# Strassen's form in a second matrix product, for two of a chunk's eight pairs of rows

## The chip, the cores and the metric

The kernel runs on one core of a Trainium2 chip. The metric is the device time of one execution in microseconds; the median of three runs of the kernel before is 2169.81 us (2168.5 to 2170.58). The profile shows one further execution. Its engines are PE (TensorE: matmuls, and PEld, its weight loads), DVE (VectorE), ACT (ScalarE), POOL (GpSimd) and SP (SyncE), whose queue issues nearly all DMAs. Matmuls write to PSUM, in banks of 2 KB per partition, 512 columns of float32.

## The reference, cut to what matters

```python
def _attn_ref(q, k, v, tau):                  # B, N, C = 4, 6080, 256
    qn = q / (norm(q, axis=1) + 1e-06);  kn = k / (norm(k, axis=1) + 1e-06)
    s = kn.transpose(0, 2, 1) @ qn / tau      # 256 x 256 for each batch, summed over N
    a = softmax(s)
    return v @ a                              # x: 24320 tokens of 256

def _moe_ref(x, w_in, w_out):                 # w_in 256 x 2048, w_out 2048 x 256
    h = x @ w_in
    g = h * (1.0 / (1.0 + np.exp(-1.702 * h)))
    return g @ w_out
```

All of it is float32; w_in and w_out arrive as float64 and are cut to float32 on the chip.

## The kernel before

For each batch the kernel multiplies a (the softmax) into w_in, so that h = v @ (a w_in). This is the first product. Tokens lie in the columns: a chunk is 1024 tokens (960 in the last one of a batch), halved into two columns of blocks of 512 (480); six chunks for each of four batches make 24. The 16 blocks of 128 rows of h are taken as 8 pairs, and a pair of row blocks, two halves of the inner 256 and two halves of the tokens are the 2 x 2 blocks of Strassen's form (Winograd's variant): 7 block products instead of 8. `unit` (L784) makes one pair: products P1 to P7 go into the banks X, Y and Z of PSUM, ACT copies partial sums out of X (`snap`, s1, u2, u4), DVE adds them (`add`, c11, c22, c21) and ACT applies the gate in place (`gate`). There are 24 x 8 = 192 units.

Every operand is split in two float32r parts, a high one (a cast) and a low one (`low`, the difference), and each block product is three matmuls: high x high, high x low, low x high. So a unit's first product has 21 matmuls.

The second product is the plain form: for each of a pair's two row blocks, each half of the tokens and each of two output blocks, three matmuls (L867) are summed in one of four banks psO0 to psO3, which a chunk holds from its first pair to its last: 24 matmuls a pair. Its operands are the gated rows' parts gh and gl, and wo_h and wo_l, which lie in SBUF for the whole run. At the end of a chunk DVE copies two of the banks and ACT the other two into the tile osb, and two DMAs store it (L889 to L901). `values` (L732) makes the seven operands of v for a chunk, `operands` (L675) those of the folded weights for a pair; the latter are kept in DRAM (w_ops) and loaded again for each unit (`weights_again`). The next batch's squares, scores and softmax run beside the products of the batch before; the first batch's stand at the start.

The order of the instructions is made by a list scheduler, `Plan.order` (L89): each node has an engine, a cost in ns, dependences, buffer slots and a due number; when an engine is free, the scheduler takes the available node of the lowest due number. `DUE` (L193) holds offsets to these numbers, `FILL` says how many blocks of the next batch's scores go beside which unit of the first chunk. Each engine then runs its list in order; so does SP's queue, in which a DMA that waits for its slot holds up what is queued behind it. The slots of one name are reused in turn: three for w_op, one for osb.

Of the kernel before, what the change touches and what calls it, by code (L numbers as in the profile page):

```python
# [11 lines left out]
F32 = mybir.dt.float32  # L12
F32R = mybir.dt.float32r
# [170 lines left out]
def dve(n):  # L184
    return (151 + n) / 0.96


def dve_fast(n):
# [10 lines left out]
}  # L199

LAG = 3200

FILL = {"gap": 10, "0": 4, "1": 3, "2": 6, "3": 0, "4": 6}
# [8 lines left out]
def channel_attention_then_glu(  # L212
# [60 lines left out]
    ident = sb.tile([P, P], F32, name="ident")  # L273
    tau_sb = sb.tile([P, 64], F32, name="tau_sb")[:, :1]
    rtau = sb.tile([P, 64], F32, name="rtau")[:, :1]
    wo_h = sb.tile([P, NF, C], F32R, name="wo_h")
    wo_l = sb.tile([P, NF, C], F32R, name="wo_l")
    win_f = dr.tile([NC2, P, DFF], F32, name="win_f")
    NK = 7
    w_ops = dr.tile([2, NU, P, NK, 2, P], F32, name="w_ops")  # L280

# [27 lines left out]
    g.add("DVE", 60, lambda: nc.vector.memset(half, 0.5), due=-8e9)  # L309
    const_i = g.add("POOL", 2000, lambda: make_identity(nc, ident), due=-9e9)  # L310
# [87 lines left out]
    wo_ready = {}  # L398

    def wout_convert(grp, words, due, slot, lows):  # L400
        t, n = to_float32(slot, lows, words, due)
        fs = slice(FG * grp, FG * (grp + 1))
        flat = lambda w: w[:, fs, :].rearrange("p f d -> p (f d)")
        h = cast(lambda: flat(wo_h), lambda: t(), FG * C, [n], [t], due + 7)
        l = low(lambda: flat(wo_l), lambda: t(), lambda: flat(wo_h), FG * C, [h], [t], due + 8)
        for f in range(FG * grp, FG * (grp + 1)):
            wo_ready[f] = l
# [3 lines left out]
    class Attention:  # L411
# [53 lines left out]
        def scores(self, us, S, due, each=25, direct=False):  # L465

            prev = None
            for n_, u in enumerate(us):
# [5 lines left out]
                if not direct:  # L474
                    hl = sbuf("hl", [P, 2, UT, 2, C], F32R, "qks")
                    part = lambda h, hl=hl, pp=pp, nt=nt: hl()[:pp, :, :nt, h, :]
                    at_ = due + each * (n_ - len(us))
                    n = cast(lambda part=part: part(0), src, w, ready, [raw, hl], at_)
                    ready = [n, low(lambda part=part: part(1), src, lambda part=part: part(0), w, [n], [raw, hl], at_ + 3)]
                for j in range(nt):  # L480
# [3 lines left out]
                    def fn(j=j, first=first, last=last, hl=hl, pp=pp):  # L484
# [19 lines left out]
                        due + (each * n_ + 3 * j if direct else j), kind="f" if direct else C,  # L504
# [25 lines left out]
        def fill(self, us, slots, due, load_due, bank_):  # L530

            for u, slot in zip(us, slots):
                self.load_unit(u, load_due, slot)
            return bank_, self.scores(us, bank_, due, 6, True), due + 6 * len(us)

        def norms(self, due):

            self.xd = xd = sbuf("acc", [P, 2, NC2, C], F32, "x_dq")
            self.rn = rn = small("rn", 2 * NC2)
            diag = lambda: xd()[:, 1, 0, :].rearrange("p (i x) -> p i x", i=NC2)  # L540
# [23 lines left out]
            self.rn_n = g.add("DVE", 800, fn_b, [a, const_i], [rn, xd], due + 4)  # L564

        def spread(self, due):

            xd, rn = self.xd, self.rn
            diag = lambda: xd()[:, 1, 0, :].rearrange("p (i x) -> p i x", i=NC2)
# [3 lines left out]
            def fn_c():  # L573
                for i in range(NC2):
                    nc.tensor.matmul(
                        pb()[:, i * P : (i + 1) * P], lhsT=ones, rhs=diag()[:, i, :], start=True, stop=True,
                    )

            c = g.add("PE", 440, fn_c, [self.rn_n], [pb, xd], due, kind="f")
# [7 lines left out]
        def softmax(self, due):  # L587
# [9 lines left out]
            for i in range(NC2):  # L597
                xi, mi, zi = (lambda i=i: xd()[:, 0, i, :]), (lambda i=i: mx()[:, i : i + 1]), (lambda i=i: zs()[:, i : i + 1])

                def fn_s(i=i, xi=xi, mi=mi):  # L600
                    nc.vector.scalar_tensor_tensor(
                        xi(), in0=S()[:, i * C : (i + 1) * C], scalar=rn()[:, NC2 + i : NC2 + i + 1], in1=self.rqb(),
                        op0=ALU.mult, op1=ALU.mult,
                    )
                    nc.vector.reduce_max(mi(), xi(), axis=AX.X)
                    nc.vector.tensor_scalar_mul(mi(), mi(), -1.0)

                e = g.add("DVE", 1000, fn_s, [*self.factors, self.last], [S, xd, rn, mx], due + 2 * i)
                e = g.add(
                    "ACT", 700 if i else 2000,  # L610
                    lambda xi=xi, mi=mi, zi=zi: nc.scalar.activation(xi(), xi(), AF.Exp, bias=mi(), accum_out=zi()),
                    [e], [xd, mx, zs], due + 2 + 2 * i,
                )

                def fn_z(xi=xi, zi=zi):
                    nc.vector.tensor_scalar_add(zi(), zi(), 1e-9)
                    nc.vector.reciprocal(zi(), zi())
                    nc.vector.tensor_scalar_mul(xi(), xi(), zi())

                z = g.add("DVE", 700, fn_z, [e], [xd, zs], due + 3 + 2 * i)  # L620

                def fn_t(i=i):
                    for j in range(NC2):
                        nc.tensor.transpose(
                            ptv()[:, j, i * P : (i + 1) * P], xd()[:, 0, i, j * P : (j + 1) * P], ident,
                        )

                ts.append(g.add("PE", 440, fn_t, [z], [xd, pt], due + 4 + 2 * i, kind="f"))
# [46 lines left out]
    def operands(at, p, w0, w1, ready, due, slot, sums):  # L675
# [13 lines left out]
        for k, z, src, deps, uses in (  # L689
# [9 lines left out]
        at.stored[p] = g.add(  # L699
            "SP", 50 + 896 * 2.6, lambda: nc.sync.dma_start(w_ops[at.b % 2, p], wt().bitcast(F32)), ok, [wt], due + 20, lag=LAG,  # L700
        )
# [30 lines left out]
    def values(b, c, turn, due, use, after=()):  # L732
# [4 lines left out]
        vt = sbuf("vt", [P, 4, HALF], F32, "v_t")  # L737
        src = vT[b, :, o : o + w].rearrange("(c p) n -> p c n", p=P)
        r = load(lambda: raw()[:, :, :w], src, 1024, after, [raw], due - 25)
        B = lambda j, n: raw()[:, j, n * hw : (n + 1) * hw]  # L740
        t = lambda i: vt()[:, i, :hw]
        t1 = tt(lambda: t(0), lambda: B(0, 1), lambda: B(0, 0), ALU.subtract, hw, [r], [raw, vt], due)
        t3 = tt(lambda: t(1), lambda: B(0, 1), lambda: B(1, 1), ALU.subtract, hw, [r], [raw, vt], due + 12)
        t2 = tt(lambda: t(2), lambda: B(1, 1), lambda: t(0), ALU.subtract, hw, [t1], [raw, vt], due + 24)
        t4 = tt(lambda: t(3), lambda: B(1, 0), lambda: t(2), ALU.subtract, hw, [t2], [raw, vt], due + 36)
        out, ok = {}, {}
        for n, (m, what, src, dep, use_) in enumerate((
            (P1, "m1", lambda: B(0, 0), r, raw),
            (P2, "m2", lambda: B(1, 0), r, raw),
            (P6, "m6", lambda: t(2), t2, vt),  # L750
            (P5, "m5", lambda: t(0), t1, vt),
            (P7, "m7", lambda: t(1), t3, vt),
            (P3, "m3", lambda: B(1, 1), r, raw),
            (P4, "m4", lambda: t(3), t4, vt),
        )):
            v = sbuf(f"v{m}{turn if m in TWICE else ''}", [P, 2, HALF], F32R, "v_op")
            at_ = due + 48 + 24 * n if m in TWICE else use + DUE[what] - 20
# [10 lines left out]
    outs = {}  # L768

    def parting(os, d, n, ob, last, o, hw, due):  # L770
# [4 lines left out]
        ns = [  # L775
            cast(lambda: to(0), lambda: src(0), h, [last], [ob, os], due, psum=True),
            g.add("DVE", dve(h), lambda: nc.vector.tensor_copy(to(1), src(1)), [last], [ob, os], due),
        ]
# [5 lines left out]
    def unit(W, V, b, c, p):  # L784
# [6 lines left out]
        begin, end = p == 0, p == NU - 1  # L791
# [52 lines left out]

        def split(h, deps, slot, by):
            gh = sbuf("gh" + slot, [P, NCH], F32R, "gh")
            gl = sbuf("gl" + slot, [P, NCH], F32R, "gl")
# [4 lines left out]
        r1 = split(h1, [g11, g12], f"1{D % 2}", cast)  # L852
        r2 = split(h2, [g2], f"2{D % 2}", cast if D < NU else cast_v)
# [175 lines left out]
```

## Time and profile before

| | |
|---|---|
| median of three runs | 2169.81 us |
| the profiled execution | 2167.3 us |
| its span, first to last instruction | 2165.5 us |
| PE busy | 2157.9 us, 9920 instructions |
| DVE busy | 1493.9 us, 2014 instructions |
| ACT busy | 1282.7 us, 1906 instructions |
| moved by DMA | 328.72 MB, mean 152 GB/s |
| clock granted to PE | full in all slices |

Busy time is the union of an engine's instructions, and matmuls overlap in the pipeline, so PE's busy time tells that it is never empty and not how fast it goes. The median lies 2.5 us above the profiled execution.

### The profile page before, as it was taken

What the parts mean: (1) busy time and instruction counts of PE and PEld (TensorE: products, weight loads), DVE (VectorE), ACT (ScalarE), POOL (GpSimd) and SP (SyncE); (2) the same over time, 40 slices, a digit from 0 to 9 for tenths busy, and PEclk for the clock granted to TensorE, in tenths of its full rate; (3) what the DMA queues carried; (4) which work ended last, traced back from release to release, by engine and by line L of the source; (5) the groups of instructions that cost most, each with busy time, mean ns of one, the idle gap of its engine ahead of it and who ended that gap; (6) DMA issues with size and microseconds to landing.
All of it is one profiled execution on the core that took longest, in us unless ns stands there. A gap on an engine that the chain in (4) does not pass through costs nothing.

```text
span 2165.5 us, 25948 instructions
## 1 busy us (share of the span) xinstructions
PE 2157.9 (100%) x9920; PEld 1811.7 (84%) x9920; DVE 1493.9 (69%) x2014; ACT 1282.7 (59%) x1906; POOL 5.7 (0%) x10
## 2 busy tenths in 40 slices
PE   9999999999999999999999999999999999999999
PEld 8888888888888888888888888888888888888887
DVE  7898677667667676776766767677677566566554
ACT  5567666656656565665665656566566555555553
POOL 0000000000000000000000000000000000000000
PEclk9999999999999999999999999999999999999999
DMA  9755445435543433433554434243355333333331
GB/s 350 291 174 197 163 154 189 140 105 196 187 162 139 141 141 116 163 122 114 205 185 148 139 131 159 101 157 120 128 194 191 112 128 117 105 126 120 105 105 54
DMA packets 88284, 328.72 MB, mean 152 GB/s; under 512 B 9312, under 2 KB 11744, under 8 KB 88160
## 3 DMA queue, kind: packets, MB, share of 16 engines
q1 hardware_dynamic: 88016, 326.93, 43.3%
q8 instruction: 78, 1.28, 0.2%
q14 instruction: 46, 0.38, 0.0%
q10 hardware_dynamic: 144, 0.13, 0.0%
HBM read 270.66 MB, written 56.36 MB: 151 GB/s over the span
## 4 chain that ended last, share of the span: by engine, by line
PE 97%; DVE 1%; DMA 1%; SPq 0%; issue 0%; ACT 0%; POOL 0%; DVEq 0%; ACTq 0%
PE ps_o L867 48%; PE ps_X L801 24%; PE ps_Y L801 12%; PE ps_Z L801 6%; PE ps_s L496 3%; PE ps_w L666 2%; PE ps_s L490 1%; DVE acc L297 1%; DMA raw_qk<-in_k 1%; DMA words<-in_w_in 0%; SPq L288 0%; DVE wf L297 0%; DVE low L378 0%; PE ps_n L549 0%; ACT wf L348 0%
## 5 line engine op out<-in xcount | busy, mean ns | idle before, releaser
L801 PE MATMUL ps_X<-v_op,w_op 128*128 128x512 f32 (+1 forms) x2304 | 625.4, 388 | 0.0
L867 PE MATMUL ps_o<-gh,wo_h 128*128 128x512 f32 (+1 forms) x1536 | 595.4, 388 | 0.0
L867 PE MATMUL ps_o<-gl,wo_h 128*128 128x512 f32 (+1 forms) x1536 | 595.1, 387 | 0.0
L867 PE MATMUL ps_o<-gh,wo_l 128*128 128x512 f32 (+1 forms) x1536 | 595.1, 387 | 0.0
L302 DVE TENSOR_TENSOR gl<-h,gh 128x1024 fp32r<-128x1024 f32 (+1 forms) x384 | 465.7, 1213 | 142.8 <-ACT gh L291 136.3
L801 PEld LDWEIGHTS ps_X<-v_op,w_op 128*128 128x128 f32 x2304 | 430.8, 188 | 86.0 <-ACT s L291 0.5
L291 ACT COPY s<-ps_X 128x512 f32<-128x512 f32 (+1 forms) x384 | 223.3, 582 | 258.8 <-PE ps_X L801 195.1
L817 ACT ACTIVATE h<-h 128x512 f32<-128x512 f32 (+3 forms) x384 | 319.5, 839 | 49.5 <-DVE h L297 49.0
L867 PEld LDWEIGHTS ps_o<-gl,wo_h 128*128 128x128 f32 x1536 | 288.3, 188 | 57.7
L867 PEld LDWEIGHTS ps_o<-gh,wo_h 128*128 128x128 f32 x1536 | 288.4, 188 | 56.7
L867 PEld LDWEIGHTS ps_o<-gh,wo_l 128*128 128x128 f32 x1536 | 288.4, 188 | 56.6
L801 PE MATMUL ps_Y<-v_op,w_op 128*128 128x512 f32 (+1 forms) x1152 | 322.4, 388 | 0.0
L801 PEld LDWEIGHTS ps_Y<-v_op,w_op 128*128 128x128 f32 x1152 | 214.9, 188 | 42.6 <-DVE h L297 0.3
L291 ACT CAST gh<-h 128x1024 fp32r<-128x1024 f32 (+1 forms) x200 | 208.4, 1042 | 53.3 <-PE ps_o L867 48.8
L294 DVE CAST gh<-h 128x1024 fp32r<-128x1024 f32 (+1 forms) x184 | 126.3, 687 | 138.4 <-ACT h L817 137.5
L291 ACT COPY u<-ps_X 128x512 f32<-128x512 f32 (+1 forms) x192 | 111.6, 581 | 177.0 <-DVE h L297 165.3
L297 DVE TENSOR_TENSOR h<-ps_Z,s 128x512 f32<-128x512 f32 (+1 forms) x192 | 131.3, 684 | 119.6 <-ACT s L291 105.0
L817 ACT ACTIVATE h<-ps_X 128x512 f32<-128x512 f32 (+1 forms) x192 | 114.0, 594 | 141.7 <-PE ps_X L801 139.3
L297 DVE TENSOR_TENSOR h<-ps_Y,u 128x512 f32<-128x512 f32 (+1 forms) x192 | 131.3, 684 | 92.7 <-PE ps_Y L801 90.0
L297 DVE TENSOR_TENSOR h<-ps_Y,s 128x512 f32<-128x512 f32 (+1 forms) x192 | 130.4, 679 | 59.9 <-ACT s L291 59.5
L801 PE MATMUL ps_Z<-v_op,w_op 128*128 128x512 f32 (+1 forms) x576 | 161.5, 389 | 0.0
L297 DVE TENSOR_TENSOR acc<-acc,sq 128x1024 f32<-128x1024 f32 (+2 forms) x96 | 112.9, 1176 | 21.5 <-ACT sq L457 19.4
(82 smaller groups left out, 1396.5 us busy)
## 6 DMA issues: line engine op xcount, KB each, us to landing
w_op<-w_ops SPq DMA_DIRECT2D x184, 896.0 KB, 4.6
raw_qk<-in_q SPq DMA_DIRECT2D x114, 256.0 KB, 5.2
raw_qk<-in_k SPq DMA_DIRECT2D x114, 256.0 KB, 5.4
w_ops<-w_op SPq DMA_DIRECT2D x32, 896.0 KB, 5.6
v_raw<-in_vT SPq DMA_DIRECT2D x20, 1024.0 KB, 7.1
out_T<-osb SPq DMA_DIRECT2D x39, 512.0 KB, 7.3
wf<-win_f SPq DMA_DIRECT2D x12, 512.0 KB, 6.4
words<-in_w_out SPq DMA_DIRECT2D x8, 512.0 KB, 6.0
```

What stands on the lines that cost most here:

```text
L291: return g.add("ACT", act(n, psum), lambda: nc.scalar.copy(dst(), src()), deps, uses, due)
L294: return g.add("DVE", dve_fast(n), lambda: nc.vector.tensor_copy(dst(), src()), deps, uses, due)
L297: return g.add("DVE", dve(n), lambda: nc.vector.tensor_tensor(dst(), a(), b(), op=op), deps, uses, due)
L302: lambda: nc.vector.tensor_tensor(dst(), src(), hi().bitcast(F32), op=ALU.subtract),
L490: nc.tensor.matmul(out, lhsT=hl()[:pp, 1, j, ci], rhs=hl()[:pp, 0, j, :], start=begin, stop=last, skip_group_check=True,)
L496: nc.tensor.matmul(out, lhsT=hl()[:pp, 1, j, l, ci], rhs=hl()[:pp, 0, j, r, :], start=begin and m == 0, stop=last and m == 2, skip_group_c ...
L666: nc.tensor.matmul(pb()[:, x * width : (x + 1) * width], lhsT=aT()[:, l, j, ci], rhs=wi()[:, r, o : o + width], start=x == 0 and n == 0, s ...
L801: nc.tensor.matmul(of(into), lhsT=wt()[:, m, l, :], rhs=v[m]()[:, r, :hw], start=begin and n == 0, stop=True, skip_group_check=True,)
L817: "ACT", act(n, psum), lambda: nc.scalar.activation(dst(), src(), AF.Gelu_apprx_sigmoid),
L867: nc.tensor.matmul(of(ob), lhsT=l[:, f, ds], rhs=rr()[:, n * hw : (n + 1) * hw], start=begin and i == 0 and m == 0, stop=end and i == 1 an ...
```

## The change

In all chunks but the first, the last two of the eight pairs (pairs 6 and 7) come first, and their second product takes Strassen's form as well. The inner 512 rows of the two pairs are split in the first and the second row block of each pair, the tokens in two halves and the output in two blocks of 128: with both pairs summed in the same banks, a block product is 3 x 2 = 6 matmuls, and there are seven. The units of these two pairs write their gated rows into two tiles of the pair of pairs, g_a and g_b; DVE makes four differences in place (one in g_t), ACT casts seven operands and DVE makes their seven low parts, all 1024 wide. P1 goes into the bank psO1 and is copied out by ACT into osb; P6, P5 and P3 are added on in the same bank, with copies after P6 and P5; P2 goes into psO0, P7 and P4 into psO2. The six other pairs are then added onto the same banks by the plain form, and at the chunk's end three of the four banks are summed with what lies in osb (DVE) and one is copied (ACT).

w_out's parts no longer stay in SBUF. The plain pairs' parts are written to DRAM once (wo_ops, 512 KB for each pair) and loaded again for each chunk (w_o); the seven operands of pairs 6 and 7 likewise (wj_ops), in three loads of 512 KB and one of 256 KB for a chunk (w_oj). All share four slots in SBUF. Three further edits go with it: `values` makes its differences in place, `spread` multiplies float32r parts, and the softmax of the batches after the first is done for both halves at once. The tables DUE, FILL are others; the core of the diff:

```diff
-    "m1": 13, "s1": -46, "m2": 16, "m6": 42, "u2": -46, "c11": -3, "g11": 22, "m5": 28, "u4": -4,
+    "m1": -16, "s1": -89, "m2": 50, "m6": 44, "u2": -64, "c11": -4, "g11": 193, "m5": 58, "u4": -39,
...
+NWO = 4
...
+    def wout_again(p, due):
+        w = wo_tile([P, 2, 2, C], "w_o")
+        return w, [load(lambda: w().bitcast(F32), wo_ops[p], 512, [wo_stored[p]], [w], due)]
...
+        for x, (k, z) in enumerate(((0, 2), (6, 7), (4, 6), (2, 4))):
+            w = wo_tile([P, 2, MS, 2, P], "w_oj")
+            n = load(lambda w=w, k=k, z=z: w()[:, : z - k].bitcast(F32), wj_ops[:, k:z], 256 * (z - k), stored, [w], due + 8 * x)
...
+            l1 = part(P1, "1", B11, G11, A, cast)
+            l2 = part(P2, "2", B21, G2, B_, cast)
+            t1 = tt(B11, B12, B11, ALU.subtract, n_, [*G12, l1], [A], at("ta"))
+            t2n = tt(T2, B22, B11, ALU.subtract, n_, [t1, *G2], [A, B_, t2], at("tb"))
+            part(P6, "6", T2, [t2n], t2, cast)
+            t3 = tt(B12, B12, B22, ALU.subtract, n_, [t1, *G2], [A, B_], at("tc"))
+            part(P7, "7", B12, [t3], A, cast)
+            part(P5, "5", B11, [t1], A, cast)
+            t4 = tt(B21, B21, T2, ALU.subtract, n_, [t2n, l2], [B_, t2], at("td"))
+            part(P3, "3", B22, G2, B_, cast)
+            part(P4, "4", B21, [t4], B_, cast)
...
+            os = out.os()
...
+            def snap(d, n, dep, what):
+                dst = lambda: os()[:, d, n * hw : (n + 1) * hw]
+                return dst, cast(dst, lambda: of(O[1]), hw, [dep], [O[1], os], at(what), psum=True)
+
+            m1 = product(P1, "1", O[1], True, [])
+            s1, s1n = snap(0, 0, m1, "k1")
+            m2 = product(P2, "2", O[0], True, [])
+            m6 = product(P6, "6", O[1], False, [s1n])
+            u2, u2n = snap(1, 0, m6, "k2")
+            m7 = product(P7, "7", O[2], True, [])
+            m5 = product(P5, "5", O[1], False, [u2n])
+            u4, u4n = snap(1, 1, m5, "k4")
+            c22 = tt(u4, lambda: of(O[2]), u4, ALU.add, hw, [u4n, m7], [O[2], os], at("kc"))
+            m3 = product(P3, "3", O[1], False, [u4n])
+            m4 = product(P4, "4", O[2], False, [c22])
...
-                if d == 0:
+                if sum_:
+                    ns.append(tt(to, src, to, ALU.add, hw, last, [ob, os], due_))
+                elif d == 0 and n == 0:
...
-            c, p = divmod(s, NU)
-            grp, a = divmod(p, PAIRS)
+            c, x = divmod(s, NU)
+            joint = b > 0 or c > 0
+            p = (x - MS) % NU if joint else x
+            grp, a = divmod(x, PAIRS)
...
+            if joint and x == MS - 1:
+                J.products(b, c, due, wj)
```

Where the instructions stand. First SP's queue at the end of a chunk of the last batch, before. w_op are the folded weights of a unit, out_T the stores of a chunk's outputs.

```order
L288 DMA v_raw_16374<-in_vT 128x2x1024 [waits DMAHW1_49,DVE_49]
L288 DMA w_op_16438<-w_ops_71 128x1792 [waits DMAHW6_49,DMAHW2_49,PE_49]
L288 DMA w_op_16522<-w_ops_71 128x1792 [waits DMAHW7_49,PE_49]
L899 DMA out_T<-osb_16502 128x1024 [waits DVE_49]
L899 DMA out_T<-osb_16502 128x1024 [waits Activation_49]
L288 DMA w_op_16600<-w_ops_71 128x1792 [waits DMAHW0_49,PE_49]
L288 DMA w_op_16672<-w_ops_71 128x1792 [waits DMAHW2_49,PE_49]
```

The same place now, on SP; w_oj and w_o are the operands of w_out.

```order
L296 DMA w_op_17159<-w_ops_70 128x1792 [waits DMAHW7_49,DMAHW6_49,PE_49]
L296 DMA w_oj_17233<-wj_ops_72 128x1024 [waits PE_49]
L296 DMA w_op_17244<-w_ops_70 128x1792 [waits DMAHW1_49,DMAHW0_49,PE_49]
L296 DMA w_oj_17312<-wj_ops_72 128x1024 [waits PE_49]
L1082 DMA out_T<-osb_16737 128x1024 [waits DMAHW2_49,DVE_49,Activation_49]
L1082 DMA out_T<-osb_16737 128x1024 [waits DMAHW3_49,DVE_49]
L296 DMA w_op_17354<-w_ops_70 128x1792 [waits DMAHW4_49,PE_49]
L296 DMA w_o_17398<-wo_ops_71 128x1024 [waits DMAHW5_49,PE_49]
```

A load of w_out's operands stands right ahead of the two stores, where a load of w_op stood before. Its slot (w_oj_17312) is the one that PE frees with the chunk's last matmul.

ACT's list at the same place, before: the copies into osb_16502 are those of the chunk's end, and the one wait for a DMA in it is for the store of the chunk before.

```order
L291 CAST gh_16495<-h1_16406 128x1024 [waits PE_49,Activation_49]
L817 ACTIVATE h1_16497<-h1_16497 128x512 [waits DVE_49]
L291 COPY osb_16502<-ps_o_15945 128x512 [waits DMAHW2_49,PE_49]
L291 COPY osb_16502<-ps_o_15956 128x512 [waits PE_49]
L291 COPY u2_16529<-ps_X_16441 128x512 [waits DVE_49,PE_49]
L817 ACTIVATE h2_16479<-h2_16479 128x1024
```

ACT's list now, at the start of the next chunk: osb_17385 is this chunk's tile, ps_o_17317 its bank psO1 after P1 and then after P6.

```order
L299 COPY u2_17356<-ps_X_17236 128x512 [waits DVE_49,PE_49]
L982 ACTIVATE h2_17301<-h2_17301 128x1024
L299 CAST gh_17364<-h1_17256 128x1024 [waits PE_49,Activation_49]
L299 COPY s1_17374<-ps_X_17236 128x512 [waits DVE_49,PE_49]
L299 COPY osb_17385<-ps_o_17317 128x512 [waits DMAHW3_49,DMAHW2_49]
L982 ACTIVATE h1_17362<-h1_17362 128x512
L299 CAST gh_17396<-g_b_17134 128x1024 [waits PE_49]
L299 COPY s1_17400<-ps_X_17308 128x512 [waits DVE_49]
L299 COPY osb_17385<-ps_o_17317 128x512 [waits PE_49]
```

The first copy into osb now stands at the start of a chunk and waits for two DMAs; a gate, a cast and a copy of other units are queued behind it. And the start of SP's queue before:

```order
L288 DMA raw_qk<-in_q 128x256 x2
L288 DMA raw_qk<-in_k 128x256
L288 DMA raw_qk<-in_q 64x256
L288 DMA raw_qk<-in_k 64x256
L288 DMA raw_qk<-in_q 128x512
```

The start of the same queue now:

```order
L296 DMA words<-in_w_out 128x2x512 x2
L296 DMA raw_qk<-in_q 128x256 x2
L296 DMA raw_qk<-in_k 128x256
L296 DMA raw_qk<-in_q 64x256
L296 DMA raw_qk<-in_k 64x256
```

Two loads of w_out's words, 512 KB each, now stand ahead of the first q and k.

## Rows read from the trace of the kernel before

**Rows 1.** The page, part 1: busy us (share of the span) and instructions.
```profile
PE 2157.9 (100%) x9920; PEld 1811.7 (84%) x9920; DVE 1493.9 (69%) x2014; ACT 1282.7 (59%) x1906; POOL 5.7 (0%) x10
```
**Rows 2.** Waits of PE, whole span: us in total, times, longest us.
```profile
PE ps_s L490 <- DMA raw_qk<-in_k: 1.1, 2, 0.6
PE ps_x L317 <- DVE half L309: 1.1, 1, 1.1
PE ps_n L549 <- DVE acc L297: 0.9, 1, 0.9
```
**Rows 3.** Chain of waits in order of time: start us, us, what.
```profile
1709.47 4.56 PE ps_o L867 x21
...
1809.59 4.76 PE ps_o L867 x21
```
**Rows 4.** Groups by line and form: count, busy us, mean ns; idle before.
```profile
L867 PE MATMUL ps_o<-gh,wo_h 128*128 128x512 f32 x1280 | 498.6, 390 | 0.0
...
L302 DVE TENSOR_TENSOR gl<-h,gh 128x1024 fp32r<-128x1024 f32 x320 | 391.6, 1224 | 114.6 <-ACT gh L291 109.2
...
L291 ACT CAST gh<-h 128x1024 fp32r<-128x1024 f32 x168 | 176.5, 1051 | 41.1 <-PE ps_o L867 37.1
...
L297 DVE TENSOR_TENSOR h<-ps_Y,s 128x512 f32<-128x512 f32 x160 | 109.6, 685 | 54.5 <-ACT s L291 54.1
...
L294 DVE CAST gh<-h 128x1024 fp32r<-128x1024 f32 x152 | 105.2, 692 | 115.4 <-ACT h L817 114.9
...
L291 ACT COPY osb<-ps_o 128x512 f32<-128x512 f32 x38 | 22.3, 586 | 11.9 <-PE ps_o L867 11.5
```
**Rows 5.** Busy us of each engine in three stretches, clock, DMA share, GB/s.
```profile
20.00:26.00 6.00, 5.50 (x27) 4.53 (x25) 4.47 (x5) 3.94 (x5) 0.00 (x0) 1.00 1.04 411
85.00:189.00 104.00, 103.97 (x493) 87.00 (x492) 89.51 (x134) 72.29 (x109) 0.00 (x0) 1.00 0.57 208
...
1749.00:1831.00 82.00, 82.00 (x365) 68.19 (x365) 48.67 (x61) 43.82 (x67) 0.00 (x0) 1.00 0.35 119
```
The columns after the stretch's length are PE, PEld, DVE, ACT, POOL.

**Rows 6.** Timeline of SP's queue: issue start us, us, DMA.
```profile
7.76 0.43 SPq L288 DMA_DIRECT2D words<-in_w_out  x1
...
532.41 0.91 SPq L899 DMA_DIRECT2D out_T<-osb  x2
...
1764.05 0.32 SPq L288 DMA_DIRECT2D w_op<-w_ops  x1
1764.42 0.90 SPq L899 DMA_DIRECT2D out_T<-osb  x2
```
**Rows 7.** out_T, issue to landing: from 520 to 545, 1755 to 1775, all.
```profile
DMA to landing us min/median/max: 2.6/3.1/3.7
...
DMA to landing us min/median/max: 7.0/8.1/9.1
...
DMA to landing us min/median/max: 2.0/7.3/9.6
```
**Rows 8.** The page, part 6: DMA issues, count, KB each, median us to landing.
```profile
w_op<-w_ops SPq DMA_DIRECT2D x184, 896.0 KB, 4.6
...
words<-in_w_out SPq DMA_DIRECT2D x8, 512.0 KB, 6.0
```
**Rows 9.** Timeline of PE, the first 50 us.
```profile
4.63 13.02 PE L490 MATMUL ps_s<-raw_qk 128*128 128x256 f32 x52
18.27 7.14 PE L490 MATMUL ps_s<-raw_qk 128*128 128x256 f32 x32 [0.62 <-DMA raw_qk<-in_k]
25.92 24.46 PE L490 MATMUL ps_s<-raw_qk 128*128 128x256 f32 x112 [0.50 <-DMA raw_qk<-in_k]
```
**Rows 10.** Timeline of the last microseconds.
```profile
2160.76 0.39 PE L867 MATMUL ps_o<-gl,wo_h 128*128 128x512 f32 x1
...
2161.19 0.37 ACT L291 COPY osb<-ps_o 128x256 f32<-128x256 f32 x1 [0.99 <-PE ps_o L867]
...
2161.59 0.42 DVE L777 COPY osb<-ps_o 128x256 f32<-128x256 f32 x1 [0.34 <-ACT osb L291]
```

More of the change, by code (lines that the diff above doesn't have):

```diff
@@ L193 @@
 DUE = {
[5 rows of a table removed]
[7 rows of a table added]
 }
 LAG = 3200
-FILL = {"gap": 10, "0": 4, "1": 3, "2": 6, "3": 0, "4": 6}
+NWO = 4
+SPLIT = {"from": 7}
+FILL = {"gap": 11, "0": 3, "1": 3, "2": 4, "3": 7, "4": 13}
 def width_cost(n):
@@ L280, in channel_attention_then_glu @@
     w_ops = dr.tile([2, NU, P, NK, 2, P], F32, name="w_ops")
+    MS = PAIRS
+    JOINT = list(range(NU - MS, NU))
+    wo_ops = dr.tile([NU - MS, P, 2, 2, C], F32, name="wo_ops")
+    wj_ops = dr.tile([P, NK, MS, 2, P], F32, name="wj_ops")
     def two(ap, w):
@@ L596, in softmax @@
             ts = []
[L597 to L612, printed above, removed]
-                )
[L615 to L628, printed above, removed]
@@ new lines, in softmax, with each @@
+            steps = [[i] for i in range(NC2)] if self.b == 0 else [list(range(NC2))]
+            def each(fn, idx):
+                return lambda: [fn(i) for i in idx]
+            for x, idx in enumerate(steps):
+                m = len(idx)
+                e = g.add("DVE", 1150 * m, each(fn_s, idx), [*self.factors, self.last], [S, xd, rn, mx], due + 2 * x)
+                e = g.add("ACT", 720 * m + (0 if x else 1350), each(fn_e, idx), [e], [xd, mx, zs], due + 2 + 2 * x)
+                z = g.add("DVE", 850 * m, each(fn_z, idx), [e], [xd, zs], due + 3 + 2 * x)
+                ts.append(g.add("PE", 220 * m, each(fn_t, idx), [z], [xd, pt], due + 4 + 2 * x, kind="f"))
@@ L673, in project, with sevens @@
         return pb, n
-    def operands(at, p, w0, w1, ready, due, slot, sums):
+    def sevens(w0, w1, ready, due, slot, sums, stored):
         (t0, v0), (t1, v1) = w0, w1
@@ L768, in channel_attention_then_glu, with gh_slot, __init__, os @@
     outs = {}
-    def parting(os, d, n, ob, last, o, hw, due):
+    gh_turn = [0]
+    def gh_slot():
+        gh_turn[0] += 1
+        return str(gh_turn[0] % 4)
+    class Outs:
+        def __init__(self, b, c):
+            self.banks = [bank(f"psO{i}", "o") for i in range(2 * NC2)]
+            self.prev = [None] * 4
+            self.also = [[], [], [], []]
+            self.sums = [False] * 4
+            self.tile = None
+        def os(self):
+            if self.tile is None:
+                self.tile = sbuf("os", [P, NC2, NCH], F32, "osb")
+            return self.tile
@@ L772, in parting @@
+    def parting(os, d, n, ob, last, o, hw, due, sum_):
         h = hw // 2
@@ L774, in parting @@
         src = lambda x: ob()[:, x * h : (x + 1) * h]
[L775 to L778, printed above, removed]
+        if sum_:
+            whole = lambda: os()[:, d, n * hw : (n + 1) * hw]
+            ns = [tt(whole, lambda: ob()[:, :hw], whole, ALU.add, hw, last, [ob, os], due)]
+        else:
+            ns = [
+                cast(lambda: to(0), lambda: src(0), h, last, [ob, os], due, psum=True),
+                g.add("DVE", dve(h), lambda: nc.vector.tensor_copy(to(1), src(1)), last, [ob, os], due),
+            ]
         dst = outT[d * P : (d + 1) * P, (B - 1) * N + o + n * hw : (B - 1) * N + o + (n + 1) * hw]
@@ L877, in unit @@
             return
-        os = sbuf("os", [P, NC2, NCH], F32, "osb")
+        os = out.os()
         for d in range(NC2):
@@ L881, in unit @@
             for n in range(2):
-                ob, last = outs[b, c][2 * d + n]
+                r = 2 * d + n
+                ob, last = out.banks[r], [out.prev[r], *out.also[r]]
+                sum_ = out.sums[r]
                 if b == B - 1 and c == NCHUNK - 1 and d == NC2 - 1:
-                    parting(os, d, n, ob, last, o, hw, due + 84)
+                    parting(os, d, n, ob, last, o, hw, due + 84, sum_)
                     continue
```

259 lines of the change are left out of this document (186 added, 73 removed), and 10 rows, old and new, of the table DUE.

## The prediction, made before the changed kernel was run

> **What bounds the kernel now.** I read the busy shares first: PE is busy for 2157.9 of 2165.5 us, DVE for 69% and ACT for 59% [rows 1]. Then the waits of PE itself: three rows, 3.1 us together, all in the start of the program [rows 2]; so nothing that DVE, ACT or a DMA does makes PE late once the first products run. Then the chain of waits in order of time, for the price of a matmul: in the steady part 21 matmuls of 512 columns take 4.76 us, 0.2267 us each, and 21 of 480 columns take 4.56 us, 0.2171 us each [rows 3]. The mean of 390 ns by form [rows 4] is the length of one in the pipeline and prices nothing, since the next one starts 0.2267 us later. The kernel's time is therefore the number of matmuls times their pitch, plus a start and a tail; and a change pays what it takes off PE, less what it makes PE wait.
>
> **The matmuls removed.** A pair's second product has 2 rows x 2 halves x 2 output rows x 3 terms = 24 matmuls; in Strassen's form it has 7 x 3 = 21. Two pairs of a chunk save 6, and all chunks but the first have the new form: 23 x 6 = 138, of which 19 chunks x 6 = 114 are 512 wide and 4 x 6 = 24 are 480 wide. 114 x 0.2267 = 25.84 and 24 x 0.2171 = 5.21: 31.05 us off PE. The order of the instructions shows the same 138 fewer on PE and no other difference of weight there (the spread matmuls of four batches, 8 small ones, change form).
>
> By the Trainium skill, "TensorE: Matmul & The Clock Gate", section "Back-to-back issue gap", an isolated warm matmul takes N/2.4 + 2.5 ns, 215.8 and 202.5 ns here, and the sum would be an estimated 29.5 us. Rows 3 say 226.7 and 217.1, and the sum above goes by them.
>
> **The elementwise work added.** Per chunk of the new form (512 wide) DVE gets 7 low parts where two pairs had 4, four differences of 1024, four sums out of PSUM where it had two copies, and loses two casts: 3 x 1.22 + 4 x 1.22 + 4 x 0.69 - 2 x 0.69 - 2 x 0.69 = 8.5 us. ACT gets 7 casts where it had 2, and four copies where it had two: 5 x 1.05 + 2 x 0.59 = 6.4 us [rows 4]. Over 23 chunks that is 197 us and 148 us, all beside PE if the engines have room. In the last batch DVE is busy for 48.67 us of an 82 us chunk, and becomes 57 of 80.6 (six matmuls fewer); in the first chunk, the tightest stretch, it has 89.51 of 104 us [rows 5] and gets a part of the next chunk's preparation and the seven forms of two pairs of w_out, some 6 us by the order: 92%. Nowhere does it pass PE, so I cost this at nothing; if its cover is gone in the first chunk, the price is at most what is added there, 6 us.
>
> **A wait that is added: the output tile.** Before, the tile osb is written at the end of a chunk only, and its store has a whole chunk to land. Now the first of Strassen's products of the next chunk, P1, is copied out of its bank into the same osb, and the bank goes on to P6 only after that copy. The copy waits for both stores of the chunk before. I count on the orders: after the last matmul of a chunk (call its end L) stand 39 matmuls up to the first one of P6 in the last batch, 39 x 0.2267 = 8.84 us; over the 23 boundaries this is 6.8 to 10.2 us, 8.84 in eight of them and 6.8 in two. Behind it must go: PE's drain, 0.2 us (a matmul's start at 2160.76 plus its pitch, to ACT's start at 2161.19 [rows 10]); the DVE sum, 0.69 [rows 4]; the issue of two stores, to about L + 1.1, since the second issue follows the first by 0.45 us [rows 6]; the landing, x; the copy, 0.59 [rows 4]; and 0.2 again for PE. So P6 is late only if x is over 8.84 - 1.1 - 0.8 = 6.9 us. What x will be no row shows, because what is queued ahead is new: a load of 512 KB (w_oj), issued at L when PE frees its slot. Two ends: with nothing ahead the two stores landed in 2.6 and 3.7 us; with a load of 896 KB issued 0.4 us ahead of them, in 7.0 and 9.1 [rows 6, 7]. I go by the share of bytes, 512/896 of the way from 3.7 to 8.1 (the middle of that pair): 6.2 us, under 6.9. Behind ACT's waiting copy stand in its queue the gate, cast and copy of other pairs, which feed PE some 2 us later, so a late landing is passed on and not gained back. I take 0.2 us for a boundary on average (the two with 6.8 us lose 1.3 each, and a few where batch loads stand ahead lose some): +4.6 us. The ends: 0, and 9.1 - 6.9 = 2.2 us each, 51 us.
>
> By the Trainium skill, "DMA: Bandwidth & Descriptors", section "Queues, rings and completion order", each DMA engine takes the descriptors of one issuing engine's ring in order. That speaks against this change, since w_oj stands ahead of the stores; rows 7 agree (7.0 to 9.1 us behind a load, against 2.6 to 3.7 with one issued after them). By it the stores pay the load's whole transfer, which the share of bytes above has in it.
>
> **Loads of w_out's operands.** SP issues 238 loads and stores more, in one queue; each waits for PE to free its slot, and what is queued behind waits with it. A slot is free on PE 6.8 us or more ahead of the operand's first use, save in four places (the first load after the P products, beside the batch's loads), where 21 matmuls or 4.7 to 4.8 us stand between. A load of 896 KB landed in 4.6 us and one of 512 KB with strided rows in 6.0 [rows 8]. I take a quarter of a microsecond each, +1; the ends are 0 and 4 x (6.0 + 0.3 - 4.7), 6.
>
> **Start and tail.** The two loads of w_out's words now go ahead of q and k: 1 MB, some 2.5 us at 411 GB/s [rows 5]. But PE waits there for data anyway: its runs of 52 and 32 matmuls end in waits of 0.6 and 0.5 us, at 17.65 and 25.41 [rows 2, 9], and the words stood at 7.76 us in the same queue [rows 6], ahead of the data that ended the second of them. One MB moves within the stretch that data bound: +0.5, ends -1 and +3. In the tail a sum of 0.69 takes the place of two half copies, 0.37 + 0.42 [rows 4, 10]: -0.1, which I leave out.
>
> **Sum.** -31.05 + 0 + 4.6 + 1 + 0.5 = -25 us. The profiled execution took 2167.3 us (span 2165.5 and 1.8 around it): 2142.3. The median of the runs shown, 2169.8, lies 2.5 above it, and on that scale I predict 2145 us.
>
> **Rivals.**
> (a) The store decides. If the stores land in over 6.9 us at every boundary, each boundary loses the excess. At 8.25 us it is 23 x 1.35 = 31: the gain is gone; beyond that the kernel is slower: at 9.1, 51 - 31 = +20, 2190 us with the other terms at nothing. For it: 7.3 us is the median of all stores before [rows 7]. Against: those had 896 KB ahead, now 512. At 7.5 us (half way to the point where it decides) 14 us go, and the time is 2154.
> (b) DVE becomes the bound where a batch's attention runs beside the products. 17 of the 23 chunks carry it; were each to lose 1 us, the time is 2162. For it: 86% in the first chunk before [rows 5], and chains through both ACT and DVE that are longer than any there was. Against: PE has no wait there today at that 86% [rows 2].
> (c) No difference: what PE loses is given back by waits of (a) and (b) together, 31 us, 2170.
> (d) Nothing waits at all, and the start gains: 2169.8 - 31 - 1 = 2138.
>
> **Chances.** The forecast with its neighbours (d) and the small form of (a), 2136 to 2156: 0.74. (b), and (a) between 7.5 and 8 us, 2156 to 2165: 0.13. (c), within 0.2% (about what a measurement of this kernel tells from no change, 4.3 us): 0.06. (a) in full, slower: 0.07. So faster 0.87, same 0.06, slower 0.07. The range reaches from (d) with a margin to most of (b): 2135 to 2162, which leaves out some 0.18.
>
> **What would show it.** In the profile after: PE with 138 matmuls fewer and the same pitch (4.76 for 21); DVE near 1690 us and ACT near 1430 us busy; PE still without rows of idle of any weight, or, if (a), idle time of PE at the P6 products, with ACT's osb copies ended by the DMA out_T, near 1 us and more each; if (b), PE's idle spread over products and ended by DVE or ACT. The time is wrong if the stores land in over 8 us, or if the pitch of the new products (the same weights twice in a row, other operands) is not 0.2267.

## The result, and the profile after

The changed kernel takes 2143.22 us (median of 4 runs, 2142.41 to 2146.37), the kernel before 2170.18 (4 runs, 2168.5 to 2170.58): a ratio of 0.988, with the interval 0.9863 to 0.9897. The prediction was 2145. The profiled execution took 2142.4 us with a span of 2140.6, 24.9 us less than before; the sum had said 2142.3.

The page after, part 1 (busy us, share, instructions), answers to [rows 1]:

```profile
PE 2131.3 (100%) x9774; PEld 1785.7 (83%) x9774; DVE 1659.3 (78%) x2199; ACT 1409.6 (66%) x2078; POOL 6.4 (0%) x10
```

PE has 146 instructions fewer: the 138, and 8 of the 16 spread matmuls. DVE's busy time rose by 165 us and ACT's by 127. The work is still what I had added up, 197 and 148: by the lengths of their instructions, added one by one, DVE has 198.0 us more (1767.3 after 1569.3) and ACT 150.4 (1523.7 after 1373.3). Neighbouring instructions overlap (ACT's copy at 1150.94 takes 0.58 us, and its next instruction starts at 1151.42), and busy time counts an overlap once.

PE's waits (us in total, times, longest), which answer to [rows 2]:

```profile
PE ps_s L535 <- DMA raw_qk<-in_q: 2.0, 1, 2.0
PE ps_o L904 <- ACT osb L299: 1.2, 2, 0.8
PE ps_x L326 <- DVE half L317: 1.1, 1, 1.1
PE ps_X L966 <- ACT u L299: 0.6, 1, 0.6
```

The waits of its weight loads show a late operand earlier, since they run ahead of the matmul; of that view one row counts here:

```profile
PEld ps_o L904 <- ACT osb L299: 2.5, 3, 1.2
```

The waits are still few, and one of them is the wait that the prediction added: a Strassen product (L904) behind the copy into osb. The 0.6 us behind u is the same wait passed on: at 211.75 us ACT starts the copy into osb after 1.20 us of waiting for out_T, and the copy u stands behind it. The price of a matmul is as before [rows 3]; the chain has, in the order start us, us, what:

```profile
358.04 2.04 PE ps_o L1046 x9
...
373.00 2.72 PE ps_o L904 x12
```

2.04 / 9 and 2.72 / 12 are both 0.2267 us, in the plain form and in the new one. (By the Trainium skill, "TensorE: Matmul & The Clock Gate", section "Back-to-back issue gap", the gap of an isolated matmul would be 0.2158; the measurement decides.)

**Where the 31.05 us went.** The timeline of PE gives the start of every run of matmuls, and the order gives what stands ahead of it. Ahead times pitch, taken from the start, is PE's lateness; I followed it through both programs. Up to 160 us it grows by 1.05 us more after than before. At chunk boundaries it does not grow before; after, it grows at seven of 23: 0.93, 0.55, 0.65, 0.68, 1.13, 0.76 and 0.82 us, 5.5 together. The rest, the changes of batch and the eight spread matmuls, comes 0.4 us cheaper. 31.05 - 1.05 - 5.5 + 0.4 = 24.9. The sum is firm, its split only to about 1 us: with the lateness read at every single matmul, and each boundary taken around its Strassen products alone, the start costs 1.2, the seven places 4.5 (the three of the store, 0.93, 1.13 and 0.82 above, 2.8 of it), and the rest is 0.5 dearer.

Three of the seven places, at the start of chunks 1, 12 and 21, end with the store. ACT's timeline of the change at the last two (start us, us, operation; in brackets the idle time before it and what ended it):

```profile
1150.94 0.58 ACT L299 COPY osb<-ps_o 128x512 f32<-128x512 f32 x1 [1.53 <-DMA out_T<-osb]
...
1917.68 0.58 ACT L299 COPY osb<-ps_o 128x512 f32<-128x512 f32 x1 [1.58 <-DMA out_T<-osb]
```

The view of out_T has the landing of these two boundaries' stores, and last that of all stores, which answers to [rows 7]:

```profile
DMA to landing us min/median/max: 6.7/7.1/7.4
...
DMA to landing us min/median/max: 6.9/7.3/7.7
...
DMA to landing us min/median/max: 2.0/5.5/7.7
```

The later of the two stores decides. Where it takes 7.4 and 7.7 us PE is late; at the usual 5.3 to 6.1 the copy waits 0.41 us at most, and PE hardly. The prediction put the point at 6.9 for a room of 8.84: chunk 21 has that room, its store lands 0.8 us over the point, and PE is 0.82 late. At chunk 1 the landing was 6.2; there the store was issued late, 1.5 us after the chunk's last matmul and not 1.1, since ACT's queue was full and its copy of the chunk's end (204.92) came late. The two long landings are not a chance of one execution: they stand at the same two boundaries in the runs words_later (7.8 and 7.9) and own_words (7.6 and 7.9) below. At chunk 21 SP issues the same DMAs as at the boundaries before and after it, so why the stores take longer there no run tells.

The start in PE's timeline:

```profile
6.83 5.80 PE L535 MATMUL ps_s<-raw_qk 128*128 128x256 f32 x14 [2.00 <-DMA raw_qk<-in_q]
```

And in the table of stretches (length, PE, PEld, DVE, ACT, POOL, granted clock, DMA share, GB/s):

```profile
6.00:8.00 2.00, 1.17 (x5) 0.83 (x6) 0.00 (x0) 0.17 (x1) 0.00 (x0) 1.00 1.09 347
8.00:10.00 2.00, 2.00 (x6) 1.18 (x7) 0.00 (x0) 1.99 (x2) 0.00 (x0) 0.59 0.99 369
10.00:12.00 2.00, 2.00 (x6) 1.17 (x5) 1.00 (x2) 2.00 (x4) 0.00 (x0) 0.50 0.51 148
...
16.00:18.00 2.00, 2.00 (x11) 1.77 (x10) 1.76 (x3) 1.49 (x3) 0.00 (x0) 1.00 1.05 405
```

The first q now comes at 6.83 instead of 4.63 us [rows 9], and after that wait PE runs for some 7 us at the lower of its two clocks, 1.2 GHz (0.50): 14 matmuls take 5.80 us. The waits at 18.27 and 25.92 [rows 9] are gone in exchange. The clock does not follow from the wait alone. The run low_planned below has the same wait and keeps the higher clock, 2.4 GHz (1.00 from 8 to 20 us):

```profile
6.83 6.75 PE L535 MATMUL ps_s<-raw_qk 128*128 128x256 f32 x28 [2.00 <-DMA raw_qk<-in_q]
```

### The profile page after: what moved, and what is told of

It reads as the page before. It is cut to its first block, busy times and chain, and to the rows that moved or that the text cites. A ratio compares the mean times of both kernels' runs of the same rounds, so it can differ in the third digit from the quotient of the medians.

```text
span 2140.6 us, 26818 instructions
## 1 busy us (share of the span) xinstructions
PE 2131.3 (100%) x9774; PEld 1785.7 (83%) x9774; DVE 1659.3 (78%) x2199; ACT 1409.6 (66%) x2078; POOL 6.4 (0%) x10
## 4 chain that ended last, share of the span: by engine, by line
PE 98%; DMA 1%; ACT 0%; SPq 0%; issue 0%; DVE 0%; ACTq 0%
PE ps_o L1046 37%; PE ps_X L966 24%; PE ps_Y L966 12%; PE ps_o L904 10%; PE ps_Z L966 6%; PE ps_s L535 4%; PE ps_s L541 3%; PE ps_w L718 2%; DMA out_T<-osb 1%; DMA raw_qk<-in_q 0%; PE ps_n L595 0%; ACT osb L299 0%; PE ps_t L667 0%; SPq L296 0%; ACT gh L299 0%
## 5 line engine op out<-in xcount | busy, mean ns | idle before, releaser
L1046 PE MATMUL ps_o<-gh,w_o 128*128 128x512 f32 (+1 forms) x2336 | 716.6, 388 | 0.0
L1046 PEld LDWEIGHTS ps_o<-gh,w_o 128*128 128x128 f32 x2336 | 436.7, 188 | 86.8
L310 DVE TENSOR_TENSOR gl<-h,gh 128x1024 fp32r<-128x1024 f32 (+1 forms) x292 | 354.2, 1213 | 149.0 <-ACT gh L299 137.8
L1046 PE MATMUL ps_o<-gl,w_o 128*128 128x512 f32 (+1 forms) x1168 | 452.7, 388 | 0.0
L982 ACT ACTIVATE h<-h 128x512 f32<-128x512 f32 (+3 forms) x292 | 240.0, 838 | 58.8 <-DVE h L305 58.4
L1046 PEld LDWEIGHTS ps_o<-gl,w_o 128*128 128x128 f32 x1168 | 219.2, 188 | 43.9
L904 PE MATMUL ps_o<-gh,w_oj 128*128 128x512 f32 (+1 forms) x644 | 222.2, 388 | 1.2 <-ACT osb L299 1.2
L904 PEld LDWEIGHTS ps_o<-gh,w_oj 128*128 128x128 f32 x644 | 120.9, 188 | 26.6 <-ACT osb L299 2.5
L966 PEld LDWEIGHTS ps_Z<-v_op,w_op 128*128 128x128 f32 x576 | 107.7, 188 | 21.2
L904 PE MATMUL ps_o<-gl,w_oj 128*128 128x512 f32 (+1 forms) x322 | 124.8, 388 | 0.0
```

The lines of the kernel that those rows point to most:

```text
L310: lambda: nc.vector.tensor_tensor(dst(), src(), hi().bitcast(F32), op=ALU.subtract),
L904: nc.tensor.matmul(of(into), lhsT=wt()[:, x, j, l, :], rhs=r()[:, j, :hw], start=begin and j == 0 and n == 0, stop=True, skip_group_check= ...
L966: nc.tensor.matmul(of(into), lhsT=wt()[:, m, l, :], rhs=v[m]()[:, r, :hw], start=begin and n == 0, stop=True, skip_group_check=True,)
L982: "ACT", act(n, psum), lambda: nc.scalar.activation(dst(), src(), AF.Gelu_apprx_sigmoid),
L1046: nc.tensor.matmul(of(ob), lhsT=wo()[:, l, i, ds], rhs=rr()[:, n * hw : (n + 1) * hw], start=first and m == 0, stop=True, skip_group_check ...
```

## Experiments

Each changes the changed kernel. In own, words_later, stores_twice, low_twice, low_behind, own_stores and own_words PE's work is the same, in the same order. Times are medians; the kernel before took 2168.6 to 2169.2 us beside them.

**own: the first copy in its own tile.**

```
-  s1, s1n = snap(0, 0, m1, "k1")          # into osb
+  s1n = cast(lambda: os1[:, :hw], lambda: of(O[1]), hw, [m1], ...)
-  ns.append(tt(to, src, to, ALU.add, ...))
+  ns.append(tt(to, src, os1 if r == 0 else to, ALU.add, ...))
```

> One edit: P1 of the Strassen form is copied into a tile of its own (2 KB a partition) and no longer into the output tile, so that this copy waits for no store; the sum at the chunk's end reads it there. The order on PE is the same. Theory (the store is what made P6 late at the start of chunks 1, 12 and 21, by 0.93, 1.13 and 0.82 us, and in part of chunk 6's 0.55): these go, some 3 us less, 2140 us, and no idle time of PE or its weight loads ended by the osb copy. Rival (the engines' queues are late there anyway, and the store's wait only stands in their place): within 1 us of 2143, with PE late at the same places behind other ACT or DVE work.

Measured: 2140.28 us (2138.34 to 2142.12), ratio 0.9865 (0.9848 to 0.9881), 2.9 us under the change. The two intervals overlap a little, but the highest of its four runs lies below the lowest of the change's (2142.41). No wait for osb is left in PE's rows:

```profile
PE ps_s L536 <- DMA raw_qk<-in_q: 2.1, 1, 2.1
PE ps_X L967 <- ACT h L983: 1.9, 1, 1.9
PE ps_X L967 <- ACT s L300: 1.1, 1, 1.1
PE ps_x L327 <- DVE half L318: 1.1, 1, 1.1
PE ps_s L536 <- ACT w L300: 0.8, 1, 0.8
```

The lateness at the boundaries of chunks 12 and 21 is gone and that of chunk 1 halved; the others stay (0.51, 0.66, 0.55, 0.92), and 0.37 comes at a place that had none. So the theory holds for three of the seven places and the rival for four. That ACT or DVE are late there with other things is read from the waits of PE's weight loads, 0.4 us and less each; no run takes these away. The profiled execution is the slowest of the four: the 1.9 us are a wait of this execution, behind a square on ACT that stood 2.76 us waiting for a load of k which took 8.83.

**words_later: w_out's words behind the first q and k.** Edit: `"w1": -178` becomes `40`.

> One edit: the two loads of w_out's words go behind the first q and k, about where they stood in the kernel before; PE's, DVE's and ACT's orders are unchanged. Theory (these loads made PE's first wait 2.0 us and the granted clock 0.5 from 8.2 to 14.6 us): the clock stays at 1.00 and PE gains the 1.05 us by which its start was behind the kernel before, 2142 us. Rival 1 (the clock is worth its whole 3.2 us): 2140. Rival 2 (PE is bound by the bytes of q and k and waits for them later): no difference, and new waits on raw_qk between 17 and 30 us.

Measured: 2142.72 us (2141.04 to 2143.11), 0.9877 (0.9863 to 0.9892): no difference from the change that these runs can tell. The first product starts at 4.62, but PE's waits have

```profile
PE ps_s L535 <- DMA raw_qk<-in_k: 3.0, 2, 2.7
```

and the table of stretches, with the granted clock after the five engines,

```profile
12.00:16.00 4.00, 1.27 (x6) 1.05 (x6) 1.43 (x3) 1.06 (x1) 0.00 (x0) 0.95 1.05 407
16.00:20.00 4.00, 4.00 (x13) 3.21 (x12) 2.56 (x3) 2.16 (x3) 0.00 (x0) 0.62 1.05 406
```

So PE waits for k a little later, and the clock falls after that wait instead (0.62). As far as the medians tell, rival 2 holds: the start is bound by bytes, at 407 GB/s, and the order of the loads decides only where the wait stands.

**stores_twice: every store twice**, the first time into a spare tensor.

```
 def store(d=d, dst=dst):
+    nc.sync.dma_start(spare[d, :, :w], os()[:, d, :w])
     return nc.sync.dma_start(dst, os()[:, d, :w])
```

> One edit: each store of a chunk's output is issued twice, once into a spare DRAM tensor ahead of the real one (1 MB more per chunk boundary on the same queue, same order on PE). Theory (the store's landing decides from about 6.9 us on): 1 MB more at some 400 GB/s puts the landing from 5.6 to about 8.2 us, some 1.3 us late at each of 23 boundaries, 30 us: 2173 us, the whole gain, with ACT's osb copies waiting for the store in nearly every chunk. Rival (a late landing is absorbed by work that stands ahead on PE): under 2150 us.

Measured: 2183.22 us (2175.3 to 2185.61), 1.0059 (1.0039 to 1.0079): slower than the kernel before. PE's waits:

```profile
PE ps_o L905 <- ACT osb L300: 25.3, 20, 2.7
```

One boundary of the last batch on SP's queue (start of the issue us, its length us):

```profile
1945.41 0.37 SPq L1085 DMA_DIRECT2D spare<-osb  x1
1945.84 0.42 SPq L1086 DMA_DIRECT2D out_T<-osb  x1
1946.35 1.06 SPq L1085 DMA_DIRECT2D spare<-osb  x1
1947.47 1.34 SPq L1086 DMA_DIRECT2D out_T<-osb  x1
```

And the copy on ACT that waits for the last of them:

```profile
1955.23 0.59 ACT L300 COPY osb<-ps_o 128x512 f32<-128x512 f32 x1 [3.20 <-DMA out_T<-osb]
```

The theory holds, and rival (a) of the prediction with it: what is queued ahead of the stores can take the whole gain. It costs 40 us and not 30, since not only the landing grows (7.7 us from 1947.47 to the copy's start at 1955.23): the issue of the last store slips too, 2.1 us behind the first where two stores have 0.45 [rows 6].

**own_stores: both.**

> Both edits together: the first copy in a tile of its own, and every store issued twice. Theory (the doubled stores cost 40 us only by the wait of the first copy; the next copy into the output tile, after P6, comes some 2.7 us later, and its room is 11 us where a landing of 8 us and issue need 10): most of the 40 goes, 2140 to 2152 us. Rival (1 MB more per boundary costs by the queue itself, late operands): 2170 us and over, with PE waiting for w_o, w_oj or w_op.

Measured: 2153.29 us (2150.92 to 2154.38), 0.9927 (0.9912 to 0.9942): 30 of the 43 us between own and stores_twice go with the first copy's wait. What is left in PE's waits:

```profile
PE ps_o L1048 <- DMA w_o<-wo_ops: 4.3, 5, 1.7
...
PE ps_o L906 <- ACT osb L301: 1.9, 3, 1.1
```

The time lies 1 us above the theory's range; the rival has a part of it, late loads of w_o behind the added bytes.

**low_twice: each low part computed twice on DVE,** DVE's list otherwise as it was.

```
+ for _ in range(2):
      nc.vector.tensor_tensor(gl, src, hi, op=ALU.subtract)
```

> One edit: each of the seven low parts of the Strassen products is computed twice on DVE (7 x 1.2 us more in 23 chunks, 195 us; same order on PE). Theory (DVE is beside PE, with 78% busy before): DVE about 1855 us, 88%, and the time within 5 us of 2143. Rival (DVE's room is used up where a batch's attention runs beside the products): 17 chunks lose 1 us or more, 2160 us and over.

Measured: 2253.03 us (2250.77 to 2257.02), 1.039 (1.0374 to 1.0405). My theory fell, by 110 us: of 181 us more on DVE PE pays more than half. PE's waits, the four longest rows:

```profile
PE ps_o L910 <- DVE gl L879: 25.9, 25, 2.0
PE ps_Y L972 <- DVE h L305: 12.2, 15, 1.6
PE ps_Z L972 <- DVE h L305: 8.1, 11, 1.6
PE ps_s L541 <- DVE qks L310: 7.6, 5, 2.1
```

Three more runs ask whether it is the low part's own delay, DVE's room, or the order.

**low_behind: as much DVE work, behind the low part.**

```
  i = nc.vector.tensor_tensor(gl, src, hi, op=ALU.subtract)
+ for _ in range(2):
+     nc.vector.tensor_tensor(idle[:, :448], idle[:, :448], idle[:, :448], op=ALU.mult)
```

> Unplanned as in low_twice, but the added DVE work (two products of 128x448 on a scratch tile that nobody reads, 1.25 us together) stands behind each low part, which is itself on time. Theory (what costs is DVE's queue: the next items for PE come 1.25 us later): 80 us or more of the 107 stay, 2225 to 2255 us, and PE waits for h, osb and g_b, no longer for gl. Rival (what costs is the low part's own delay, 25.9 us of PE's listed waits and those that follow from them): under half stays, 2195 us or less.

Measured: 2245.72 us (2242.15 to 2248.24), 1.0351 (1.0334 to 1.0368). In PE's waits those for gl shrink and those for h take their place:

```profile
PE ps_Y L975 <- DVE h L306: 13.7, 15, 1.8
PE ps_Z L975 <- DVE h L306: 13.1, 14, 2.1
...
PE ps_o L913 <- DVE gl L880: 4.0, 7, 0.7
```

So it is not the late operand itself; all that stands behind in DVE's queue is late.

**low_planned: the same work as low_twice, known to the planner.**

```
  l = low(gl, src, hi, n_, [n], ...)
+ l = low(gl, src, hi, n_, [l], ...)
```

> As low_twice, the seven low parts twice (195 us of DVE more), but the planner that writes out the order knows of the second one, so that PE's order and the other engines' fit it. Theory (DVE has room for it, and low_twice lost 107 us because an order fitted to DVE's durations was kept while they grew): at most a third of the 107 is left, under 2180 us. Rival (DVE's room is used up, whatever the order): 2230 us and over.

Measured: 2230.38 us (2227.12 to 2232.0), 1.0282 (1.0267 to 1.0297): the rival's side, though only just. The stretches tell more than the sum (after the length: PE, PEld, DVE, ACT). First low_behind in the last batch:

```profile
1760.00:2100.00 340.00, 328.16 (x1426) 266.53 (x1425) 254.26 (x332) 195.80 (x292) 0.00 (x0) 0.99 0.49 170
```

Then low_planned, in its last batch and in a stretch with attention (the granted clock is the number after POOL):

```profile
1840.00:2180.00 340.00, 340.00 (x1499) 280.98 (x1498) 269.29 (x313) 209.21 (x307) 0.00 (x0) 1.00 0.53 179
...
200.00:400.00 200.00, 191.34 (x798) 152.10 (x797) 171.89 (x195) 130.83 (x187) 0.00 (x0) 0.96 0.62 219
```

In the last batch, without attention, planned work leaves PE no idle time at 79% of DVE, and unplanned work leaves it 12 of 340 us at 75%. With attention beside it DVE stands at 86%, and PE is idle for 8.7 of 200 us though the work was planned; the granted clock of 0.96 takes another 8. The change itself has there, and in a stretch that begins in its first chunk,

```profile
200.00:400.00 200.00, 199.43 (x879) 164.52 (x878) 168.98 (x198) 147.04 (x209) 0.00 (x0) 1.00 0.69 242
...
100.00:300.00 200.00, 199.32 (x905) 165.18 (x904) 176.41 (x248) 151.30 (x225) 0.00 (x0) 1.00 0.70 246
```

84.5% and 88%, with next to no loss. So the order is a real cause: in the last batch as much work costs nothing once the planner knows of it. That DVE's room is used up beside attention is not shown. A share of 86% is one that the change carries; by PE's instructions (798 against 879) DVE would be at an estimated 95% if PE were on time, which leaves little room; but low_planned's due numbers were fitted to other durations, and an order that does not fit leaves PE idle for 7.4 of 200 us in such a stretch at 73% (old_numbers, next). A table fitted to the doubled low parts would tell the two apart; none was run. Some 7 to 11 us of the losses of the three runs are the clock, an estimate from its mean in their profiled executions, 0.993 to 0.995 against the change's 0.998.

**old_numbers: the changed kernel with the due numbers of the kernel before** for the steps that both have; no instruction differs.

> The changed kernel with the due numbers of the kernel before for every step that both have; the work is the same to the instruction, only the order differs. Theory (DVE's added work costs nothing only because the order was fitted to it; one_pair, low_twice and low_planned lost 50 to 107 us without a fit): PE waits for DVE and ACT in every chunk, 2180 us or more, no gain left. Rival (the count of matmuls decides, and an order worth a few us is found from either table): 2143 to 2155 us.

Measured: 2198.38 us (2197.74 to 2199.95), 1.0136 (1.0119 to 1.0153). The new steps keep their numbers, so this mix was fitted to neither kernel. The order alone is worth 55 us here, twice the change's gain. PE's waits:

```profile
PE ps_X L966 <- ACT s L299: 12.0, 18, 1.4
PE ps_X L966 <- DVE s_sum L562: 5.1, 2, 2.6
```

A stretch in the middle:

```profile
1400.00:1600.00 200.00, 192.58 (x876) 157.34 (x875) 145.76 (x190) 126.25 (x181) 1.01 (x1) 0.98 0.48 169
```

PE is idle for 7.4 of 200 us with DVE at 73%. The last batch, without attention, costs nothing even in this order:

```profile
1800.00:2140.00 340.00, 340.00 (x1502) 281.35 (x1501) 238.45 (x286) 210.68 (x307) 0.00 (x0) 1.00 0.51 182
```

**one_pair: Strassen's form for one pair of a chunk.** Edit: `MS = PAIRS` becomes `MS = 1`.

> Strassen's form for one pair of a chunk instead of two (the sums out of the banks are as many, the products half as deep). Theory (the time is the number of matmuls times their pitch, and the sums and copies cost PE nothing): 69 matmuls come back, 57 x 0.2267 + 12 x 0.2171 = 15.5 us, 2158.7 us, give or take 3 for another order. Rival (each chunk of the new form has a price of its own on PE, near the 5.5 us of boundary waits or more): the shorter products give less time to the sums, and PE waits for them: 2165 us and over.

Measured: 2212.01 us (2200.98 to 2215.46), 1.019 (1.0163 to 1.0218): the theory misses by 53 us. PE's waits, in the profiled execution, which was the fastest of the four (2200.98):

```profile
PE ps_o L904 <- ACT osb L299: 11.4, 20, 1.2
PE ps_Z L966 <- DVE h L305: 6.7, 5, 2.0
```

P1, P6, P5 and P3 go through one bank, with a copy by ACT between them; with one pair a product is 3 matmuls long and not 6, and PE waits for the copy in 20 places. That is the rival. The waits listed for it are 11.4 us; how much of the 53 us is an order that was not fitted to one pair, the run does not tell apart.

**plain_dram: the plain form, operands from DRAM.** Edit: `MS = 0`, `joint = False`, all eight pairs loaded again, due numbers of the kernel before.

> The second product in its plain form for all pairs, with w_out's operands loaded from DRAM as in the change (24 matmuls for two pairs again; due numbers of the kernel before, with those of the two new steps). Theory (the form took 31.05 us off PE and the loads cost next to nothing): back to the kernel before, 2166 to 2173 us, no wait of PE for w_o to speak of, DVE back near 1490 us. Rival (the loads cost several us that the Strassen form had to pay first): 2176 us and over, with PE waiting for w_o.

Measured: 2171.94 us (2171.52 to 2175.11), 1.0017 (1.0007 to 1.0026). The theory holds: loads, start and a slightly other order cost 2.7 us (1.5 to 5.6), and PE has no wait for w_o among its rows. Strassen's form is then worth 2171.9 - 2143.2 = 28.7 us. Its page, part 1:

```profile
PE 2159.5 (99%) x9912; PEld 1811.1 (83%) x9912; DVE 1484.2 (68%) x2003; ACT 1295.8 (60%) x1934; POOL 5.7 (0%) x10
```

**own_words: own and words_later together.**

> The two edits that took something off, together: the first copy in its own tile, and w_out's words behind the first q and k. Theory (independent: 3 us of store waits and 0.5 us of the start): 2139 to 2140 us, under both kernels. Rival (the start only moves its wait): as own, 2140.3 us, not below it.

Measured: 2139.95 us (2138.24 to 2141.41), 0.9865 (0.985 to 0.988). Under both kernels, and level with own: the start gives nothing that these runs can tell.

## Why the prediction was right, and where it was not

- **Matmuls removed, 31.05 us:** right. The pitch in the new form is 0.2267, PE has the 138 matmuls fewer, and plain_dram gives 28.7 us for the form with its boundary waits inside.
- **Elementwise work, 0:** right as a number, wrong in its reason. I put the busy time beside the stretch's length, found 92% at most (it became 88%) and called it room. low_behind leaves PE idle for 12 of 340 us at 75% and old_numbers for 7.4 of 200 at 73%, while the change loses nothing to speak of at 88%. What hides DVE's work is an order in which each result is due before PE comes to it; the share tells only that such an order can exist. That the order of this kernel is one was not worked out in the prediction, so on this term the number was luck. Whether DVE's room runs out with 8 us more per chunk stays open.
- **Output tile, 4.6 us:** the mechanism was right, the size too large for the store alone. I had 6.2 us of landing and 0.2 us for each boundary; it was 5.5 (median of all stores; usually 5.3 to 6.1 for the later of two), and three boundaries of 23 with a landing of up to 7.7, or ACT's queue just full, lost 2.9 together, most of which own took away. The two boundaries with only 6.8 us of room lost 0.68 and 0.76 and not 1.3, their later stores landed in 4.6 and 4.3 us, and their rows name ACT's and DVE's own work. Together the boundaries cost 4.5 to 5.5 us, since the other engines' lateness, which the sum had at nothing here, makes up for what the store did not cost: that the term fits is luck. Two slips stand in its working. The pieces up to the issue, 0.2 + 0.69 + 0.45, add up to 1.34 and not 1.1; the trace of the change has 1.1 at chunk 21, so the point of 6.9 stands. And the landing is taken between the upper end of one pair (3.7) and the middle of the other (8.1); between the two upper ends, which are the later stores, it is 6.8, next to the point itself. The point at which the store decides was right: stores_twice.
- **Loads of w_out, 1 us:** no wait of PE for w_o or w_oj in the changed kernel. plain_dram's 2.7 us contain what they cost in all.
- **Start, 0.5 us:** 1.05. That PE may run part of the start at the lower clock was not in the term; it does so in the change's profiled execution and not in all others with such a wait (last section). words_later shows that another order of the loads only moves the wait.
- **Rivals:** (a) is real and stands one queued megabyte away. (b) I priced at 2162 us and held unlikely; in the change it did not come, but lateness of DVE's results is the nearest limit: 8 us more of DVE per chunk cost 87 to 110 us. (c) and (d) did not occur.

## What to carry to other kernels

When one engine never waits, the saving is its instructions times their pitch, and the risk lies in the order of the others, not in their busy share: ask what happens when one of their items is late by a microsecond. A tile that is now written at the start of a stage instead of its end inherits the landing time of the last store; a small tile of its own removes that wait. After such a change the numbers that set the order must be fitted anew; here, the older numbers cost twice what the change gains.

## What the runs showed of the hardware

A wait of 2.0 us in PE's first 7 us was followed by some 7 us at a granted clock of 0.50, and in words_later a wait of 2.7 us, which ended at 14.81 us, by a clock of 0.62 from 16 to 20 us. This is no fixed price of such a wait: low_planned and one_pair have the same first wait (2.00 and 2.02 us) and stay at 1.00, and so does own_words after a wait of 2.55 us that ends at 14.76; what decides between the two, no run shows. The waits of 0.6 and 0.5 us at the start of the kernel before left the clock at 1.00. A DMA's issue is not of fixed length: in stores_twice it took 0.37 us for the first of four stores in a row and 1.34 for the last.
